# A convolution and a multiplicative feed-forward on one core: the first side task gets another tile, fewer sums, and a later place for its first product

## The chip, the cores and the metric

The kernel runs on one core of a Trainium2 chip. The metric is the time of one execution in microseconds of device time; where several executions were timed, the median is given. TensorE is PE in the profile, VectorE DVE, ScalarE ACT, GpSimd POOL, SyncE SP. A name such as L454 is line 454 of the kernel's file.

## The reference

x has the shape 8 x 3904 x 192, `weight` 8 x 7, and the four matrices of the feed-forward are 192 x 1024 (w1 and w2), 1024 x 1024 (w3) and 1024 x 192 (w_out). Each of 8 heads owns 24 of the 192 channels; its seven taps go through a softmax, and each channel is a causal sum of seven neighbouring tokens:

```
out[b, s, h, g] = sum_k softmax(weight)[h, k] * x_pad[b, s + k, h, g]
a = y @ w1;  b = y @ w2;  h = (a * b) @ w3;  result = h @ w_out
```

Here y is the convolution's result as 31232 rows of 192. Sums of the convolution start anew at the head of each of the 8 sequences.

## The kernel before, in words

**Rounds.** The 31232 tokens are two halves of 15616 (`NS = 2`), which run side by side: a half sits on 64 of the 128 partitions. A half is cut into 31 rounds R of 512 tokens, the last one shorter. w3 and w_out are multiplied together once (`w3_turn`, `w3_product`), into `W_sb`, so a round has two parts. `first_product(R)` (line 512) makes the products a and b for eight blocks of 128 columns, `pa` and `pb` in PSUM; ACT evicts `pa` (line 519) and DVE multiplies it with `pb` (line 521) into `abT`. `second_product(R, r)` multiplies `abT` with `W_sb` (line 537) for one half; ACT evicts the result into `osb` (line 542), and a DMA on SP's queue stores it. All of them take PSUM tiles from one pool of four (`banks`).

**Phases.** The order is written out by hand. Rounds 0 to 2 come first, with the conversion of the weights between them. Then phase p holds the first products of two rounds, and behind these the four second products of two earlier rounds. Phase 0 has only second products (rounds 0 and 1); phase 1 begins with rounds 3 and 4. Between the second products stand convolution units (`convolve`) where `places` names the phase and the position.

**Two ways to the convolution.** For most rounds the convolution is a banded matrix product on PE (`conv`, line 323), evicted as `convo` (line 332), stored as rows to DRAM (`store`, line 361) and brought back transposed into `xT` (`transposes`, line 395), all on SP's DMA queue. For six phases (`SIDE = (3, 7, 8, 11, 12, 14)`) it is done beside PE instead. There are 18 side tasks, three groups of 64 channels for each such phase. For task i, `side_cast` (line 438, POOL's queue) writes x in bf16 to DRAM, `side_transpose` (line 448, SP's queue) brings it transposed into a raw tile of 1040 columns, `side_first` (line 454, ACT) makes the product with one tap into the accumulator `acc_of[i % 2]`, and six sums on DVE (line 472) add the other taps, the last of them writing the operand `side_of`. The operand must be complete when the first products of its phase begin.

**Tiles of the side tasks.** Five raw tiles rotate. Four lie in the two places of the turned w3 tiles (`raw_of[0]` to `raw_of[3]`), the fifth behind the operand tile in the place of the first w3 load (`raw_of[4]`). The two accumulators lie in the places of two more w3 loads. So none of them is free before the weights have been worked up, which ends in round 2.

**The plan.** A loop gives each phase some sums (`room`: 8 where the phase has convolution units, else 7) and fills them in task order; a task may be split over two phases. Casts and transposes of a task are placed one phase ahead of its first product: the transposes of `starts[p + 1]` stand on SP's queue behind the first products of phase p. The first product of a task carries a number n: it is issued at the head of the n-th of the phase's four second products, and the sums behind it are issued from there on (`side_steps`). Every engine and every DMA queue runs its instructions in the order in which they were issued.

**Around the end of round 2** the order on SP's queue is: the taps, the transposes of the tasks of phase 0, the store of block 3 (rows that round 3 and round 4 need), the transposes of these two rounds into `xT`, and then the transposes of the tasks of phase 1. On POOL's queue, `later_loads` issues the weights, the casts of phase 0's tasks, the x rows of block 4, the casts of phase 1's tasks, and part of block 5. A DMA on SP's queue also waits for the eighth one before it to have landed.

Of the kernel before, what the change touches and what calls it, by code (L numbers as in the profile page):

```python
# [16 lines left out]
def kernel(  # L17
# [19 lines left out]
    NS = 2  # L37
# [31 lines left out]
    t0 = (LAG + 3) * CH  # L69
# [36 lines left out]
    rows_c = dram.tile([TS, NP, NS * Q], BF16, name="rows_c")  # L106
# [14 lines left out]
    def group(r, e):  # L121
        return slice((2 * r + e) * C, (2 * r + e) * C + C)
# [55 lines left out]
    for r in range(NS):  # L178
        p = group(r, 0).start
# [12 lines left out]
        out=diag, in_=diag, pattern=[[-1, 128 + 8]], compare_op=ALU.is_equal,  # L192
# [13 lines left out]
    for i in range(4):  # L206
        d = diag[i * C:i * C + C, i * C + 2 * i:i * C + 2 * i + C]
        nc.vector.tensor_copy(
            out=cmask[i * C:i * C + C],
            in_=bass.AP(tensor=d.tensor, offset=d.offset, ap=[d.ap[0], [1, 2], [1, C]]))  # L210
# [40 lines left out]
    for i in range(3):  # L251
# [3 lines left out]
        out=share[:, :, 0:K], in0=taps.unsqueeze(1).to_broadcast([H, H, K]), scalar=total,  # L255
        in1=diag[0:H, 0:H].unsqueeze(2).to_broadcast([H, H, K]), op0=ALU.mult, op1=ALU.mult)
    spread = banks("spread")
    for i in range(4):
# [6 lines left out]
        out=wsb, in_=spread[:, 0, 0:2 * H].rearrange("p (h k) -> p h k", h=H)  # L265
# [5 lines left out]
        out=cprod.rearrange("p h k (s two) -> p h k s two", two=2),  # L271
# [6 lines left out]
    p = group(1, 0).start  # L278
# [3 lines left out]
    for k in range(2):  # L282
# [5 lines left out]
                          in_=bps[:, 0, 0:C * H].rearrange("p (h s) -> p h s", s=C))  # L288
# [110 lines left out]
    HALO = 16  # L399
# [12 lines left out]
    def side_span(p):  # L412
        return (2 * p + 1) * CH, min((2 * p + 3) * CH, TS)

    tasks = [(q, k) for q in SIDE for k in range(NP)]
    side_of, acc_of, raw_of = {}, [], []
# [27 lines left out]
    def side_transpose(i):  # L444
        p, k = tasks[i]
        t0, t1 = side_span(p)
        for lo, hi in ((t0 - HALO, t0 + CH), (t0 + CH, t1)):
            nc.sync.dma_start_transpose(
                out=raw_of[i % 5][:, HALO + lo - t0:HALO + hi - t0], in_=rows_c[lo:hi, k, :])

    def side_first(i):
        p, k = tasks[i]
        t0, t1 = side_span(p)
        nc.scalar.activation(  # L454
            out=acc_of[i % 2][:, 0:t1 - t0], in_=raw_of[i % 5][:, HALO - 1:HALO - 1 + t1 - t0],
            func=ACT.Copy, scale=wC[:, k, K - 2:K - 1])

    def side_sums(i):
        p, k = tasks[i]
        t0, t1 = side_span(p)  # L460
        starts = [z for z in range(0, TS, S) if t0 <= z < t1]

        def job(d, last):
            def run():
                raw, acc = raw_of[i % 5], acc_of[i % 2]
                if d == 2:
                    for z in starts:
                        nc.vector.memset(acc[:, z - t0:z - t0 + 1], 0.0)
                for lo, hi in [(t0, t1)] if last else \
                        zip([t0] + [z + d for z in starts], starts + [t1]):  # L470
                    a = acc[:, lo - t0:hi - t0]
                    nc.vector.scalar_tensor_tensor(  # L472
                        out=side_of[p][:, k, 0:t1 - t0] if last else a,
                        in0=raw[:, HALO + lo - t0 - d:HALO + hi - t0 - d],
                        scalar=wC[:, k, K - 1 - d:K - d], in1=a, op0=ALU.mult, op1=ALU.add)
            return run
        size = (t1 - t0) / (2 * CH)
        return [(size, job(d, d == 0)) for d in list(range(2, K)) + [0]]
# [151 lines left out]
    for k in (0, 2, 1):  # L630
# [6 lines left out]
    places = {0: (0, 1), 1: (2,), 2: (0, 1, 2), 3: (0,), 4: (0,), 6: (0, 2), 7: (0, 2),  # L637
              10: (0,), 11: (0,)}
    starts, chain, room, p = {}, {}, 0, -1
    for i, (q, k) in enumerate(tasks):  # L640
        for cost, f in side_sums(i):
            while room < cost:
                p += 1
                room = 8 if p in places else 7
                at, free = 0, 0
                starts.setdefault(p, [])
            if not chain or chain[max(chain)][-1][0] != i:
                starts[p].append(i)
                n = min(2 * NS - 1, -int(-free * 0.48))
                chain.setdefault(p, []).append((i, n, lambda i=i: side_first(i)))  # L650
            assert p < q
            room, at = room - cost, at + cost
            chain.setdefault(p, []).append((i, None, f))
        free = at
    for p in starts:
        for i in starts[p]:
            assert i < 5 or p < 2 or max(v for v in chain if chain[v][0][0] <= i - 5) <= p - 2
# [20 lines left out]
    def later_loads():  # L678
# [12 lines left out]
        for f in x_jobs(5, 0):  # L691
# [16 lines left out]
        4: seq((w3_product, 4), (w3_product, 6),  # L708
               (conv, 3, 96, 96, (A,), (0,)), (conv, 3, 96, 96, (V,), (1,)),
               (A, wC[Q:128], wC[0:Q]), (side_tiles,), *[(side_transpose, i) for i in starts[0]],  # L710
               (store, 3), (transposes, 3), (transposes, 4))})

# [31 lines left out]
    for p, rounds in enumerate(phases):  # L744
# [16 lines left out]
        for i in starts.get(p + 1, ()):  # L761
            side_transpose(i)
# [44 lines left out]
```

## Time and profile before

| | |
|---|---|
| median of 3 runs | 518.94 us (517.76 to 519.64) |
| the profiled execution | 520.86 us, of which 519.2 are the span |
| PE busy | 510.7 us (98%) |
| DVE busy | 446.5 us (86%) |
| ACT busy | 353.3 us (68%) |
| POOL busy | 87.4 us (17%) |
| mean granted clock of TensorE | 0.997 |

The span runs from the first instruction to the last one of the profiled execution. Rows of a timeline give the start, the time taken, the engine and the line, what is written and read with its shape, how many instructions are merged, and in brackets how long the engine had been idle and what ended it. SPq is SP's DMA queue: its times are those of issuing, not of the transfer. A row of a window gives for each engine its busy time, then the granted clock, the share of the DMA engines and the GB/s. A row of a DMA queue gives packets, MB and a share of busy time.

### The profile page before, as it was taken

The page shows a single profiled execution, that of the slowest core. Times are in us where ns is not written, and L with a number is a line of the kernel's source. Part 1 is how long each engine was busy: PE and PEld are TensorE (multiplying, and loading weights), DVE is VectorE, ACT ScalarE, POOL GpSimd, SP SyncE. Part 2 cuts the span into 40 slices and gives each one's busy share as a digit, 9 for nine tenths or more (in the row PEclk, how much of TensorE's full clock was granted, in tenths as well). Part 3 has the DMA queues.
Part 4 walks back from the last instruction along what each step waited for, and adds up shares of the span by engine and source line. Part 5 has one row for each costly group of instructions (what it writes and reads, how often), then busy time and mean ns, then how long its engine had stood idle before and what let it go on. Part 6 is the DMA issues. An engine that isn't in the chain of part 4 may idle for free.

```text
span 519.2 us, 14128 instructions
## 1 busy us (share of the span) xinstructions
PE 510.7 (98%) x6020; PEld 336.4 (65%) x6020; DVE 446.5 (86%) x430; ACT 353.3 (68%) x403; POOL 87.4 (17%) x178
## 2 busy tenths in 40 slices
PE   8999889999999999999999999999999999999997
PEld 4446845846658476485765847658585585856777
DVE  6898679999899898989989899898998989989580
ACT  6886647577876776747777675684767667576462
POOL 9875013050030211302112021100000000000000
PEclk9999989999999999999999999999999999999999
DMA  9999959899697968937457499744013072210304
GB/s 143 150 154 173 162 126 213 158 138 120 134 174 144 156 84 179 155 101 80 58 114 55 107 175 172 152 59 133 7 56 100 2 181 64 64 61 3 123 2 153
DMA packets 154189, 59.46 MB, mean 115 GB/s; under 512 B 108945, under 2 KB 154125, under 8 KB 154125
## 3 DMA queue, kind: packets, MB, share of 16 engines
q0 software_dynamic: 66912, 17.07, 36.7%
q1 hardware_dynamic: 87053, 41.38, 35.6%
q8 instruction: 47, 0.77, 0.6%
q14 instruction: 17, 0.14, 0.1%
q10 hardware_dynamic: 160, 0.10, 0.1%
HBM read 34.42 MB, written 34.88 MB: 133 GB/s over the span
## 4 chain that ended last, share of the span: by engine, by line
PE 92%; DMA 3%; ACT 2%; DVE 1%; SPq 1%; issue 0%
PE pa L512 30%; PE pb L512 30%; PE ops L537 28%; DMA rows<-convo 2%; PE cps L323 2%; PE wps L605 1%; ACT asb L519 1%; ACT convo L332 1%; DVE abT L521 1%; PE warm L233 1%; SPq L395 1%; DMA xT<-rows 1%; DMA out_dram<-osb 0%; PE ops L558 0%; PE tps L385 0%
## 5 line engine op out<-in xcount | busy, mean ns | idle before, releaser
L521 DVE TENSOR_TENSOR abT<-asb,pb 128x1024 bf16<-128x1024 bf16 x240 | 292.5, 1221 | 45.3 <-ACT asb L519 27.4
L519 ACT CAST asb<-pa 128x1024 bf16<-128x1024 f32 x244 | 247.0, 1013 | 67.3 <-PE pa L512 66.9
L512 PEld LDWEIGHTS <-wn 64*128 64x128 bf16 x1488 | 139.0, 95 | 85.7 <-issue 3.6
L512 PEld LDWEIGHTS <-ws 64*128 64x128 bf16 x1488 | 131.1, 94 | 73.0 <-issue 3.3
L537 PE MATMUL ops<-W_sb,abT 128*128 128x192 bf16 x1936 | 164.8, 247 | 0.2 <-ACT convo L332 0.2
L537 PEld LDWEIGHTS <-abT 128*128 128x128 bf16 x1936 | 158.3, 98 | 8.0 <-issue 7.6
L512 PE MATMUL pa<-xT,wn 64*128 64x512 bf16 x456 | 124.1, 378 | 2.0 <-DMA xT<-rows 0.9
L512 PE MATMUL pb<-xT,wn 64*128 64x512 bf16 x456 | 125.2, 379 | 0.0
L512 PE MATMUL pa<-xT,ws 64*128 64x512 bf16 x456 | 124.2, 379 | 0.3 <-DMA xT<-rows 0.3
L512 PE MATMUL pb<-xT,ws 64*128 64x512 bf16 x456 | 123.0, 379 | 0.0
L542 ACT COPY osb<-ops 128x768 f32<-128x768 f32 (+1 forms) x61 | 48.6, 796 | 82.0 <-PE ops L537 82.0
L472 DVE SCALAR_TENSOR_TENSOR acc<-raw,wC,acc 128x1024 f32<-128x1024 bf16 (+3 forms) x100 | 93.9, 973 | 1.3
L512 PE MATMUL pb<-side,wn 64*128 64x512 bf16 (+1 forms) x288 | 75.0, 368 | 0.2 <-DVE abT L521 0.2
L512 PE MATMUL pa<-side,wn 64*128 64x512 bf16 (+1 forms) x288 | 74.5, 368 | 0.0
L512 PE MATMUL pa<-side,ws 64*128 64x512 bf16 (+1 forms) x288 | 74.4, 368 | 0.0
L512 PE MATMUL pb<-side,ws 64*128 64x512 bf16 (+1 forms) x288 | 73.7, 368 | 0.0
L749 POOL COPY pace<-abT 1x2 bf16<-1x2 bf16 x46 | 8.0, 174 | 221.8 <-DVE abT L521 221.8
L332 ACT CAST convo<-cps 128x640 bf16<-128x640 f32 (+2 forms) x62 | 34.1, 633 | 1.8 <-PE cps L323 1.7
L157 POOL DMA_DIRECT2D xb<-in_x_dram x46 | 30.3, 663 | 9.6 <-issue 6.4
L438 POOL DMA_DIRECT2D rows_c<-in_x_dram x36 | 27.4, 763 | 9.7 <-issue 8.9
L472 DVE SCALAR_TENSOR_TENSOR acc<-side,wC,acc 128x1024 f32<-128x1024 bf16 (+6 forms) x20 | 19.5, 1013 | 1.9 <-ACT acc L454 1.6
L454 ACT ACTIVATE acc<-raw,wC 128x1024 f32<-128x1024 bf16 (+1 forms) x15 | 16.8, 1117 | 4.5 <-DMA raw<-rows_c 4.5
(68 smaller groups left out, 126.2 us busy)
## 6 DMA issues: line engine op xcount, KB each, us to landing
out_dram<-osb SPq DMA_DIRECT2D x58, 384.0 KB
xb<-in_x_dram POOLq DMA_DIRECT2D x28, 240.0 KB, 7.0
rows_c<-in_x_dram POOLq DMA_DIRECT2D x30, 130.0 KB, 3.8
rows<-convo SPq DMA_DIRECT2D x13, 120.0 KB
rows<-convo SPq DMA_DIRECT2D x6, 240.0 KB
xb<-in_x_dram POOLq DMA_DIRECT2D x6, 228.0 KB, 8.2
w3b<-in_moe_w_dram POOLq DMA_DIRECT2D x4, 256.0 KB, 5.6
w3b<-in_moe_w_dram POOLq DMA_DIRECT2D x8, 128.0 KB, 5.8
```

Source lines behind the costliest of these rows:

```text
L157: nc.gpsimd.dma_start(out=tiles[js[0]][0][group(r, e), s:s + w, :], in_=bass.AP(tensor=x.tensor, offset=(r * TS + t - PAD) * D, ap=[[D, C] ...
L323: nc.tensor.matmul(o.rearrange("p (w g) -> p w g", g=wd)[:, :, c - c0:c1 - c0], Aband[group(r, e), h, :], xb[group(r, e), s:s + m, c:c1], ...
L332: f(out=convo[:, e::E, k, :, lo:lo + c] .rearrange("p w r g -> p r w g"), in_=src[:, :, :, o:o + c])
L438: nc.gpsimd.dma_start(out=rows_c[t0 - HALO:t1, k, r * Q:r * Q + Q], in_=x_rows[r * TS + t0 - HALO:r * TS + t1, k * Q:k * Q + Q])
L454: nc.scalar.activation(out=acc_of[i % 2][:, 0:t1 - t0], in_=raw_of[i % 5][:, HALO - 1:HALO - 1 + t1 - t0], func=ACT.Copy, scale=wC[:, k, K ...
L472: nc.vector.scalar_tensor_tensor(out=side_of[p][:, k, 0:t1 - t0] if last else a, in0=raw[:, HALO + lo - t0 - d:HALO + hi - t0 - d], scalar ...
L512: nc.tensor.matmul(p[:, r, f * N:f * N + N], w_of(i, k, r)[rs, ft * 128:(ft + 1) * 128], operand(R, k, rs), start=(k == 0), stop=(k == NP ...
L519: nc.scalar.copy(out=asb[:, :, 0:per * N], in_=pa[:, :, 0:per * N])
L521: nc.vector.tensor_tensor(out=ab[:, f0, :, 0:N], in0=asb[:, :, 0:N], in1=pb[:, :, 0:N], op=ALU.mult)
L537: nc.tensor.matmul(ops[:, g // 2, (g % 2) * D:(g % 2) * D + D], ab[:, jt, r, g * 128:(g + 1) * 128], W_sb[:, jt, :], start=(jt == 0), stop ...
L542: nc.scalar.copy(out=osb.rearrange("p (a g) d -> p a (g d)", g=2), in_=ops[:, 0:ng // 2, 0:2 * D])
L749: P(out=pace, in_=abT_of[R][0:1, ft, 1, 0:2])
```

## The change

Three edits, all in the side tasks.

```
-                out=raw_of[i % 5][:, HALO + lo - t0:HALO + hi - t0], in_=rows_c[lo:hi, k, :])
+                out=raw_of[i % 5 - 1][:, HALO + lo - t0:HALO + hi - t0], in_=rows_c[lo:hi, k, :])
...
-                room = 8 if p in places else 7
-                at, free = 0, 0
+                room = 5 if p == 0 else 8 if p in places else 7
+                at, ends = 0, {}
...
-                n = min(2 * NS - 1, -int(-free * 0.48))
+                n = max(p == 0, -(-ends.get(i - 2, 0) // 2))
...
-        free = at
+        ends[i] = at
```

The index `i % 5 - 1` stands in `side_first` and `side_sums` too. It shifts the rotation by one: task 0 takes `raw_of[4]`, in the place of the first w3 load, and tasks 1 to 4 take the four tiles in the places of the turned w3.

Phase 0 gets five sums instead of eight. So it holds only task 0, without its last sum; its transposes are the only side transposes ahead of the store of block 3, and those of tasks 1 and 2 come one place later on SP's queue, behind the transposes of rounds 3 and 4. On POOL's queue the casts of task 1 move behind the x rows of block 4. Every later sum moves back by three, so that phases 8 and 12 hold other tasks than before, and the last sums of task 14 and of task 17 are now the last ones of phases 11 and 13.

The number n of a task's first product came from the number of sums that the phase had taken before it. It is now half of the number of sums at which the task before last, which has the same accumulator, ended within this phase, and 0 where that task ended earlier. In phase 0 it is at least 1. By this, all products stand at the head of their phase, but for task 0 (ahead of the second of phase 0's second products) and tasks 2 and 6 (at the same place in phases 1 and 4).

PE's instructions and their order are the same.

More of the change, by code (lines that the diff above doesn't have):

```diff
@@ L454, in side_first @@
         nc.scalar.activation(
-            out=acc_of[i % 2][:, 0:t1 - t0], in_=raw_of[i % 5][:, HALO - 1:HALO - 1 + t1 - t0],
+            out=acc_of[i % 2][:, 0:t1 - t0], in_=raw_of[i % 5 - 1][:, HALO - 1:HALO - 1 + t1 - t0],
             func=ACT.Copy, scale=wC[:, k, K - 2:K - 1])
@@ L464, in run @@
             def run():
-                raw, acc = raw_of[i % 5], acc_of[i % 2]
+                raw, acc = raw_of[i % 5 - 1], acc_of[i % 2]
                 if d == 2:
```

## The prediction

> **What bounds the kernel now.** I read the page's span, engine shares and clock row first, then the chain that ended last, and then the timeline of the stretch in which that chain leaves TensorE (PE).
>
> ```profile
> span 519.2 us, 14128 instructions
> ```
>
> ```profile
> PE 510.7 (98%) x6020; PEld 336.4 (65%) x6020; DVE 446.5 (86%) x430; ACT 353.3 (68%) x403; POOL 87.4 (17%) x178
> ```
>
> ```profile
> PEclk9999989999999999999999999999999999999999
> ```
>
> PE is busy for 98% of the span, so the time moves only where PE waits or runs at a lower clock. The clock row has one dip, in the sixth slice (65 to 78 us). The chain's longest pieces (start, us, what) give the clean length of a phase and the place where PE leaves the chain; the row after them is the timeline's, the start of phase 0:
>
> ```profile
> 53.84 9.53 DMA rows<-convo
> 91.47 8.03 PE ops L537 x96
> ...
> 220.81 10.67 PE ops L537 x128
> 252.31 2.75 PE ops L537 x32
> ...
> 285.09 2.75 PE ops L537 x32
> ...
> 317.50 10.66 PE ops L537 x128
> ```
>
> ```profile
> 52.45 2.82 PE L537 MATMUL ops<-W_sb,abT 128*128 128x192 bf16 x32
> ```
>
> From the second products of phase 5 (220.81), which have no convolution unit among them, to those of phase 6 (252.31) it is 31.50 us: 10.67 for the four and 20.83 for the pair of first products. Phase 0 has two convolution units of 0.7 each more (row below), so 12.1 and 20.83. It began at 52.45; undisturbed, the second products of phase 1 would start at 85.4. They start at 91.47: **6.1 us are lost here**, and nearly nothing later. Where, by the timelines of PE, ACT and SP's DMA queue:
>
> ```profile
> 59.13 0.22 PE L323 MATMUL cps<-xb,Aband 32*32 32x120 bf16 x2 [0.46 <-ACT osb L542]
> 60.05 0.70 PE L323 MATMUL cps<-xb,Aband 32*32 32x120 bf16 x62 [0.69 <-ACT convo L332]
> ...
> 67.28 0.37 PE L512 MATMUL pa<-xT,wn 64*128 64x512 bf16 x1 [0.87 <-ACT osb L542]
> ...
> 68.01 0.37 PE L512 MATMUL pa<-xT,ws 64*128 64x512 bf16 x1 [0.33 <-DMA xT<-rows]
> ...
> 69.32 0.37 PE L512 MATMUL pa<-xT,wn 64*128 64x512 bf16 x1 [0.92 <-DMA xT<-rows]
> ```
>
> ```profile
> 57.24 1.15 ACT L454 ACTIVATE acc<-raw,wC 128x1024 f32<-128x1024 bf16 x1 [4.53 <-DMA raw<-rows_c]
> 58.30 0.78 ACT L542 COPY osb<-ops 128x768 f32<-128x768 f32 x1
> 58.98 1.94 ACT L332 CAST convo<-cps 128x640 bf16<-128x640 f32 x4
> ```
>
> ```profile
> 46.36 5.85 SPq L448 DMA_TRANSPOSE raw<-rows_c  x4
> 52.33 8.54 SPq L361 DMA_DIRECT2D rows<-convo  x8
> 61.06 0.31 SPq L354 DMA_DIRECT2D rows<-convo  x1
> 63.39 7.08 SPq L395 DMA_TRANSPOSE xT<-rows  x5
> ```
>
> Two things hold PE. First, the side product of task 0 stands ahead of the first eviction in ACT's queue and waits 4.53 us for its raw tile. The eviction runs only at 58.30, PE runs out of PSUM tiles, and the second unit is through at 60.75 instead of about 58.5: 2.3 us. Second, round 3's operand is late. The store of its rows starts at 52.33 behind four side transposes, a part of it lands 9.53 us after 53.84, and only then do the transposes into xT start (63.39; the third has landed when PE goes on at 69.32). The waits ended at 67.28, 68.01 and 69.32 come to 2.1 us. (The first is put down to an eviction; the tile it needs was free by then, so I read it as xT's first landing.) Then the clock is down, 70 to 72 in the window view:
>
> ```profile
> 70.00:72.00 2.00, 2.00 (x14) 0.80 (x10) 1.00 (x1) 0.76 (x1) 0.00 (x0) 0.50 0.33 74
> ```
>
> The granted clock, third from the end, is 0.50. The pace of the matmuls says that this lasts from 69.5 to 72.8, so some 1.6 us are lost. 2.3 + 2.1 + 1.6 = 6.0, which closes on the 6.1.
>
> **The change, part by part.** *Raw tile of task 0 in w3's first place.* Its first transpose now waits until 46.36 for a turned w3 tile to be multiplied. The new place is free after the second turn, and then the two casts decide:
>
> ```profile
> 38.95 1.24 DVE L594 STREAM_TRANSPOSE w3T<-w3b 128x1024 f32<-128x1024 f32 x1
> ...
> 48.39 1.22 DVE L332 CAST convo<-cps 128x320 bf16<-128x320 f32 x2 [1.45 <-PE cps L323]
> ```
>
> ```profile
> L438 POOL DMA_DIRECT2D rows_c<-in_x_dram x2: 793/795/797, 35.1 to 35.9; - x2
> ```
>
> ```profile
> DMA to landing us min/median/max: 8.1/8.1/8.2
> ```
>
> The turn ends at 40.19, the second cast lands at 35.9 + 8.1 = 44.0, and both casts keep their place in POOL's order. So the transposes go out at 44.0, 2.4 us sooner.
>
> *Five sums in phase 0, so only task 0 is fetched ahead.* Two of the four side transposes leave the queue ahead of the store. The other two hold SP for half of 5.85 us, to 47.0; the store then waits only for its data, evicted by 49.61 (48.39 + 1.22), and starts 2.7 us sooner. When it lands is the one large unknown. Queue rows (packets, MB, busy share) of 48 to 50, where SP's queue has no row at all, and of 50 to 52:
>
> ```profile
> q0 software_dynamic: 1872, 0.33, 210.6%
> ```
>
> ```profile
> q0 software_dynamic: 1068, 0.26, 132.8%
> q1 hardware_dynamic: 348, 0.09, 33.4%
> ```
>
> So the transposes issued from 46.36 on moved nothing before 50. Call T the moment at which the transposes into xT can go out (63.39 now). Early end: packets start 4 us after issue as now, at 48, move at some 200 per us, about 1,040 for two transposes (0.27 MB at 0.09 for 348), until 53.2; the 0.39 MB of the four stores that round 3 needs follow at the same packet rate with rows of 768 bytes (2.5 us), and I allow 1.4 us until they count as landed: T = 57.1. Late end: nothing moves before 50.5 whatever is queued, the two transposes end at 55.7, and the stores get only 0.12 MB per us (3.2 us): T = 60.3. The third operand is there 69.32 - 63.39 = 5.9 later, at 63.0 to 66.2. PE, undisturbed, wants it at 52.45 + 12.1 + 0.43 = 65.0, since four matmuls of a group precede it. I take the middle, 64.6, which costs nothing, and charge 0.4 us for the late half.
>
> *The product behind the first eviction.* ACT would evict at about 55.3, cast the first unit by 58.1 and then run the product, 1.15 us. Its tile is there even if it lands as late as now, 57.24. The second unit finds its PSUM tiles free. The five sums behind the product end near 66, when the first eviction of round 3 is made. Were that cover gone, each sum too many would cost its own 1.3 us.
>
> *What moves elsewhere.* Task 1's casts go behind the four x loads of block 4 on POOL: these loads get earlier, and the tile is wanted in phase 1 only. Tasks 1 and 2 put four transposes behind those into xT, where task 2's two stood, so half of 5.85 more stands ahead of the output stores, block 4's store and round 5's transposes:
>
> ```profile
> 90.69 6.96 SPq L395 DMA_TRANSPOSE xT<-rows  x4
> ```
>
> Round 5's third transpose was out by 90.69. With 4.7 less from T, 2.9 more and 4 to land it is there by 92.9, and PE now wants it at about 96.5: hidden, with over 3 us left.
>
> *Later products, and sums that end later.* A product now goes out as soon as its accumulator is free, mostly at the head of a phase, where ACT idles before the first eviction. In phase 6 one stands ahead of the last eviction: 252.31 to 285.09 takes 32.78 us, against 32.41 for phase 7 (to 317.50) with as many units. Those 0.37 us go. In return, three sums have slid back through the schedule, and task 14's last sum becomes the eighth of phase 11, wanted at once by phase 12:
>
> ```profile
> 414.32 5.24 DVE L472 SCALAR_TENSOR_TENSOR acc<-side,wC,acc 128x1024 f32<-128x1024 bf16 x4
> ```
>
> ```profile
> 424.18 0.75 PE pa L512 x6
> ```
>
> Eight at 5.24 / 4 = 1.31 from 414.32 end at 424.8; PE wants the result at 424.18 + 0.43 = 424.6: 0.2 us lost. Phase 13 has nine sums of 768 columns at its end, three quarters as long (8.8 us, begun about 1.6 after PE's second products): inside their 10.67, nothing lost.
>
> **The sum.** 6.1 + 0.37 - 0.2 - 0.4 = 5.9 us, against the profiled execution's 520.86 (519.2 of span and 1.7 around it). That one stood 1.9 above the median of the runs, 518.94; the gain is taken as the same there: **513.0**.
>
> **The rivals.**
>
> *A: part of the operand's lateness stays.* For it: 9.53 us from issue to landing is far more than a store's own packets. Against it: two transposes fewer ahead of it. With T at 61.2, PE waits 2.1 us at 65.0. If the clock falls again as at 70 to 72, 1.6 more goes: gain 6.3 - 2.1 - 1.6 = 2.6, 516.3; without that, 4.2 and 514.7. In the rows the dip followed three short waits, broken by matmuls, so I price A with the dip. [...]
>
> *B: the store is held by the software queue, not by the transposes ahead of it.* For it: nothing moved for SP in 48 to 50 beside that queue's 1872 packets. Then T stays near 63.4, PE arrives at 64.6 and is held to 69.32 as now, with the dip: the front gains nothing, 0.37 less 0.2 is left: 518.8. Against it: in 50 to 52 both queues moved, and what SP's moved were transposes, not the store. [...]
>
> *C, slower: the raw tile comes late, now behind the first eviction.* There it holds the second eviction, the second unit's casts and the PSUM tile of the fourth second product, due at 61.8. If the tile lands at L, PE goes on at L + 1.15 + 0.78, a loss of L - 59.9. That equals today's 6.1 at L = 66.0 and is slower by over 0.3% from 67.6; at 69 the time is 521.8. Against it: L is 57.24 now, with a later issue.
>
> **How the numbers follow.** The forecast (T up to about 60) has 0.68, A 0.18, B 0.09, C 0.05. About 0.3%, 1.6 us, is what a measurement of this kernel can tell. Faster are the forecast and A, 0.86; the same is B, 0.09; slower is C, 0.05. The forecast's own range is 511.7 to 514.7: gains of 6.3 to 5.1 between the ends of T, and 0.9 either way as the three runs spread. Reaching over A's priced end with some spread: 511.7 to 516.8.
>
> **What would show it.** Right: task 0's product on ACT follows the first eviction near 58 with no wait; the store starts near 49.7; the transposes into xT go out by 60.3; PE's waits at 59.13 and 67.28 are gone, no slice has a lower clock, and phase 1's second products start near 85.6. Phase 6 to 7 takes 32.4. Wrong: transposes into xT still near 63, a wait for raw behind the first eviction, or PE held by a side sum at the head of phase 12 or 14 for over 1 us.

## The result and the profile after

The changed kernel takes 515.82 us (median of 6 runs, 515.41 to 517.49) against 518.80 for the kernel before in the same comparison: a ratio of 0.9948, with a 95% interval of 0.9930 to 0.9966. It is faster by 3.0 us. The time lies inside the prediction's outer range, 511.7 to 516.8, but above the forecast's own, 511.7 to 514.7, and the gain is half of the 5.9 us forecast. By the number alone it would be taken for rival A (514.7 to 516.3); the rows below say otherwise. Its profiled execution took 516.07, with a span of 514.4.

On the page, PE is busy for 99% of the span, and the dip of the granted clock is gone:

```profile
PE 508.4 (99%) x6020; PEld 335.9 (65%) x6020; DVE 446.5 (87%) x430; ACT 353.6 (69%) x403; POOL 87.7 (17%) x180
```

```profile
PEclk9999999999999999999999999999999999999999
```

The timelines of SP's queue, ACT and PE around phase 0, in that order, and the chain's piece that begins phase 1's second products:

```profile
43.64 2.52 SPq L448 DMA_TRANSPOSE side<-rows_c  x2
50.53 3.19 SPq L361 DMA_DIRECT2D rows<-convo  x8
57.32 0.32 SPq L354 DMA_DIRECT2D rows<-convo  x1
59.63 8.73 SPq L395 DMA_TRANSPOSE xT<-rows  x6
```

```profile
56.14 0.80 ACT L542 COPY osb<-ops 128x768 f32<-128x768 f32 x1 [2.58 <-PE ops L537]
56.84 1.96 ACT L332 CAST convo<-cps 128x640 bf16<-128x640 f32 x4
58.64 1.19 ACT L454 ACTIVATE acc<-side,wC 128x1024 f32<-128x1024 bf16 x1
59.69 0.83 ACT L542 COPY osb<-ops 128x768 f32<-128x768 f32 x1
```

```profile
53.29 2.81 PE L537 MATMUL ops<-W_sb,abT 128*128 128x192 bf16 x32
56.03 0.73 PE L323 MATMUL cps<-xb,Aband 32*32 32x120 bf16 x64
56.69 2.81 PE L537 MATMUL ops<-W_sb,abT 128*128 128x192 bf16 x32
59.44 0.72 PE L323 MATMUL cps<-xb,Aband 32*32 32x120 bf16 x64
60.10 5.45 PE L537 MATMUL ops<-W_sb,abT 128*128 128x192 bf16 x64
```

```profile
86.38 8.03 PE ops L537 x96
```

The reader is to see three things. The product (L454) runs behind the first eviction with no wait. Two transposes instead of four stand ahead of the store, and those into xT go out at 59.63. PE has no bracket left in this stretch: phase 0 begins at 53.29 and phase 1's second products at 86.38, **33.09 us** later, where the profiled execution before had 39.02. In this front part the waits are gone as forecast.

The rest of the two traces, by the same starts of second products (32.78 and 32.41 for phases 6 and 7 before):

```profile
247.28 2.75 PE ops L537 x32
...
279.70 2.75 PE ops L537 x32
...
312.48 10.67 PE ops L537 x128
```

Phase 6 to 7 takes 32.42 now, so the 0.37 went there; but 7 to 8 takes 32.78, so it came back. From phase 10 to 12 it is 64.74 (375.48 to 440.22) against 64.51 before: 0.23 lost at task 14's last sum. And phase 0 begins 0.84 later in this execution (53.29 against 52.45). 5.93 + 0.36 - 0.37 - 0.23 - 0.84 = 4.85, the difference of the two spans, 4.8. The late start is not the work of the instructions that were moved: it stands in the chain ahead of them all, as the landing of the first load of x; PE's first convolution waits 0.84 us for it, and the later rounds keep that distance:

```profile
2.31 4.90 DMA xb<-in_x_dram
...
7.25 0.71 PE cps L323 x61
```

So the two profiled executions differ by what was forecast, less 0.4 in phase 7 and a late start; the medians differ by 3.0. The question for the experiments is which of the two tells the truth, and which of the edits carries it.

### The profile page after: what moved, and what is told of

Its sections match the earlier page's. It is cut to its first block, busy times and chain, and to the rows that moved or that the text cites. A ratio compares the mean times of both kernels' runs of the same rounds, so it can differ in the third digit from the quotient of the medians.

```text
span 514.4 us, 14129 instructions
## 1 busy us (share of the span) xinstructions
PE 508.4 (99%) x6020; PEld 335.9 (65%) x6020; DVE 446.5 (87%) x430; ACT 353.6 (69%) x403; POOL 87.7 (17%) x180
## 4 chain that ended last, share of the span: by engine, by line
PE 93%; DVE 3%; ACT 1%; DMA 1%; issue 1%; POOL 0%; POOLq 0%
PE pa L512 30%; PE pb L512 30%; PE ops L537 30%; PE cps L323 2%; DVE acc L472 1%; DVE abT L521 1%; PE wps L605 1%; DMA xb<-in_x_dram 1%; ACT asb L519 1%; ACT convo L332 0%; DVE side L472 0%; PE ops L558 0%; PE tps L385 0%; PE tps L370 0%; POOL xb L157 0%
## 5 line engine op out<-in xcount | busy, mean ns | idle before, releaser
L512 PE MATMUL pb<-xT,ws 64*128 64x512 bf16 x456 | 121.7, 376 | 0.0
L472 DVE SCALAR_TENSOR_TENSOR acc<-raw,wC,acc 128x1024 f32<-128x1024 bf16 (+3 forms) x90 | 88.4, 1014 | 1.2
L472 DVE SCALAR_TENSOR_TENSOR acc<-side,wC,acc 128x320 f32<-128x320 bf16 (+13 forms) x30 | 24.9, 879 | 0.3
L472 DVE SCALAR_TENSOR_TENSOR side<-raw,wC,acc 128x1024 bf16<-128x1024 bf16 (+1 forms) x14 | 17.4, 1246 | 0.5
```

Of the source, the lines that this page charges most:

```text
L472: nc.vector.scalar_tensor_tensor(out=side_of[p][:, k, 0:t1 - t0] if last else a, in0=raw[:, HALO + lo - t0 - d:HALO + hi - t0 - d], scalar ...
L512: nc.tensor.matmul(p[:, r, f * N:f * N + N], w_of(i, k, r)[rs, ft * 128:(ft + 1) * 128], operand(R, k, rs), start=(k == 0), stop=(k == NP ...
```

## The experiments

Each was timed in five rounds beside the kernel before. "Phase 0" below means the time from the start of its second products to those of phase 1, read from the trace as above; without any wait it is 33.1. "xT at" is the time at which SP issues the first transpose into xT. A median is to be read beside that of the kernel before in the same comparison: 518.49 for e1 to e4, 518.37 for e5 to e8, 518.64 for e9 to e11, 518.51 for e12. The ratio is an estimate over all executions, so it is not exactly the quotient of the two medians.

| kernel | median us | ratio to before, 95% | phase 0 | xT at |
|---|---|---|---|---|
| before, profiled at first | 518.80 | | 39.02 | 63.39 |
| e1, before again | 518.08 | 0.9991 (0.9968 to 1.0013) | 35.98 | 61.36 |
| e2, tile only | 517.25 | 0.9974 (0.9954 to 0.9994) | 34.91 | 61.21 |
| e3, five sums only | 517.27 | 0.9972 (0.9949 to 0.9995) | 34.86 | 59.87 |
| e4, product behind only | 520.41 | 1.0030 (1.0010 to 1.0049) | 38.07 | 61.87 |
| changed | 515.82 | 0.9948 (0.9930 to 0.9966) | 33.09 | 59.63 |
| e9, changed again | 515.44 | 0.9929 (0.9905 to 0.9953) | 33.08 | 57.50 |
| e5, changed, product first | 515.61 | 0.9941 (0.9919 to 0.9963) | 33.21 | 57.92 |
| e6, changed, old tile | 515.85 | 0.9966 (0.9945 to 0.9986) | 33.08 | 59.24 |
| e7, changed, eight sums | 518.09 | 0.9992 (0.9976 to 1.0008) | 36.20 | 61.23 |
| e12, changed, two tasks ahead | 517.66 | 0.9972 (0.9945 to 0.9999) | 34.26 | 61.21 |
| e8, changed, six sums | 515.32 | 0.9936 (0.9914 to 0.9958) | 33.54 | 57.49 |
| e10, e8 again | 515.21 | 0.9924 (0.9898 to 0.9950) | 33.54 | 58.87 |
| e11, changed, old places later on | 515.74 | 0.9934 (0.9910 to 0.9958) | 33.08 | 57.52 |

### e1: the kernel before, once more

No edit.

> The kernel before, unchanged, to see how its executions spread and what phase 0 costs in another profiled one. Theory D: the 6.1 us that phase 0 lost in the profiled execution were a dear draw; 1.6 of them, the low clock behind the waits, come only in some executions. Then executions with a mean clock of 1.000 take 517.5 to 519, those at 0.997 take 520 to 521, and in a profiled execution at 1.000 the second products of phase 1 start about 37.4 us after those of phase 0 instead of 39.0. Rival S: phase 0 loses about 6 in every execution (39.0 in the new profile too, whatever the clock), and the changed kernel gives some 2 to 3 us back elsewhere in most executions.

Its profiled execution took 517.73, with a mean clock of 1.000. Timelines of ACT, SP and PE, the chain, and a window (granted clock third from the end):

```profile
56.88 1.15 ACT L454 ACTIVATE acc<-raw,wC 128x1024 f32<-128x1024 bf16 x1 [4.31 <-DMA raw<-rows_c]
```

```profile
61.36 8.18 SPq L395 DMA_TRANSPOSE xT<-rows  x6
```

```profile
52.30 2.81 PE L537 MATMUL ops<-W_sb,abT 128*128 128x192 bf16 x32
```

```profile
67.81 0.37 PE L512 MATMUL pa<-xT,wn 64*128 64x512 bf16 x1 [0.34 <-DMA xT<-rows]
```

```profile
88.28 8.03 PE ops L537 x96
```

```profile
68.00:72.00 4.00, 4.00 (x40) 2.20 (x38) 3.40 (x4) 3.04 (x3) 0.13 (x1) 1.00 0.44 99
```

The wait of ACT is the same (4.31 against 4.53), but the transposes into xT go out 2.0 us sooner than in the first profile, PE waits less for them, and the clock stays at full speed. Phase 0 costs 35.98, so **2.9 us over the clean 33.1, not 6**. Theory D had said 37.4, so even it saw too little of the spread. (This execution is one of the quicker ones: the median of its twelve is 518.08.) Over the 98 executions of the kernel before in these comparisons for which a clock is known, most lie between 517.3 and 519.1 at a mean clock of 1.000; in 21 the clock was 0.997 or lower, and nearly all of these took 519 to 523. The execution that the prediction was made from, 520.86 at 0.997, is not among the 98, but it is of the same kind as the 21. Rival S, a loss of about 6 us in every execution, falls.

### e2, e3, e4: each edit alone, on the kernel before

```
e2:  raw_of[i % 5]  ->  raw_of[i % 5 - 1]
e3:  room = 8 if p in places else 7  ->  room = 5 if p == 0 else 8 if p in places else 7
e4:  n = min(...)  ->  n = max(p == 0, min(...))
```

> The kernel before with the raw tiles shifted by one and nothing else: task 0 in w3's first place, both tasks still fetched ahead of the store. Theory (two causes: ACT's wait and the lateness of round 3's operand): the product no longer waits behind the raw tile, but four transposes stay ahead of the store, so the transposes into xT go out at 61 to 62; PE waits some 2 us there; 1 to 2 us faster than before. Rival O (only the operand's chain sets the end, and the number of transposes sets it): no faster than before by more than 0.5 us. Rival P (ACT's wait alone was the loss): as fast as the changed kernel, 3 us faster than before.

> The kernel before with five sums in phase 0 and nothing else: only task 0 is fetched ahead of the store, in its old tile, and its product stays ahead of the first eviction. Theory: the transposes into xT go out near 60 instead of 63.4, but ACT still waits for the raw tile until 56 to 57, so PE comes to round 3 some 2 us late: 1.5 to 2.5 us faster than before. Rival O: as fast as the changed kernel. Rival P: no faster than before by more than 0.5 us.

> The kernel before with task 0's product behind the first eviction and nothing else. Theory: PE no longer waits at 59 to 61, but the transposes into xT still go out at 63.4 and PE waits for them to 69.3 as before, now in one piece of some 4 us instead of several: within 0.7 us of before, rather slower if the longer wait brings the low clock each time (up to 1.6). Rival P: 2.3 us faster.

In e2 the product no longer waits, and the transposes into xT stay at 61.21. It is 1.2 us faster, as the two causes said. Its trace has one oddity, a stop of PE inside the fourth second product with no releaser in the profile. PE comes to round 3 only at 66.6 because of it, so a wait for xT may be hidden behind it; what the stop is stays open:

```profile
65.89 0.82 PE L537 MATMUL ops<-W_sb,abT 128*128 128x192 bf16 x8 [1.43 <-issue]
```

In e3 it is the other way round: the transposes go out at 59.87, and ACT still waits:

```profile
57.27 1.15 ACT L454 ACTIVATE acc<-raw,wC 128x1024 f32<-128x1024 bf16 x1 [4.60 <-DMA raw<-rows_c]
```

That leaves 34.86 - 33.1 = 1.8 us, the price of ACT's wait where the operand is early. The median is 1.2 us under before, less than the 1.5 to 2.5 expected (the interval reaches from 0.3 to 2.6). In e4 ACT's wait is gone and the operand is about as late as in e1 (transposes into xT at 61.87, not at the 63.4 expected). PE now waits for it almost in one piece, 0.54 and then 2.71 us, and the half clock follows:

```profile
68.87 0.58 PE L512 MATMUL pa<-xT,wn 64*128 64x512 bf16 x1 [2.71 <-DMA xT<-rows]
```

```profile
69.00:71.00 2.00, 2.00 (x12) 0.74 (x11) 1.14 (x3) 1.01 (x1) 0.00 (x0) 0.50 0.35 78
```

10 of e4's 12 executions were at 0.997 or lower, and it is **slower than before**, by 0.1 to 0.5% (1.9 us in the median; at most 1.6 had been expected). Beside e1, the four second products end 1.5 us sooner after phase 0's start (12.25 against 13.75), but the waits for xT come to 3.25 us instead of 1.05, and the clock takes more. So rival P, the ACT wait alone, falls by e2 and e4, and rival O, the operand alone, by e3: the intervals of e2 and e3 do not reach the 3 us of all edits together.

Both causes have to go. In e4, where only ACT's wait goes, the result is worse than nothing. e2 is not a second test of this: its early tile sends two of the four side transposes at 42.75, and the store begins at 50.22, where e4 has 46.56 and 52.32. So the tile helps the operand too.

### e5, e6: the changed kernel, one edit undone

```
e5:  n = max(p == 0, -(-ends.get(i - 2, 0) // 2))  ->  n = -(-ends.get(i - 2, 0) // 2)
e6:  raw_of[i % 5 - 1]  ->  raw_of[i % 5]
```

> The changed kernel with task 0's product back ahead of the first eviction of phase 0, all else as changed. Theory (the raw tile, sent early and with one task only, is there before ACT is free): in the changed kernel's trace the packets of the two transposes end near 52 and ACT is free at 53.6, so the product runs without a wait and the time is that of the changed kernel within 0.4 us; its place is worth nothing once the tile is early. Rival P (its place is what removes the stall): 1.5 to 2.3 us slower than the changed kernel, with an ACT wait on the raw tile of over 1 us in the trace.

> The changed kernel with the raw tiles in their old rotation: task 0's transposes wait for the turned w3 tile again (46 to 47 instead of 44). Theory: the product, behind the first eviction, is still covered (raw there at 57, wanted at 58.6); the stores stand behind transposes that end 2 us later, the transposes into xT go out near 60 to 60.5, the third operand is there about when PE wants it: 0 to 0.8 us slower than the changed kernel. Rival O (the earlier tile is what pulls the operand's chain forward): 2 us slower or more, with PE waiting on xT.

In e5 the product runs at the head of phase 0 without a wait:

```profile
52.84 1.15 ACT L454 ACTIVATE acc<-side,wC 128x1024 f32<-128x1024 bf16 x1
```

Phase 0 is 33.21 and the median that of the changed kernel. In e6 the transposes start at 46.24 again, the product behind the eviction is covered, and its profiled execution has the clean 33.08. So the tile and the place do the same work for ACT: with one task fetched ahead, either is enough. They are perhaps not quite equal. In e6, 5 of 12 executions took 517.5 to 519.5; in e5 none of 6 went above 515.9, and of the 12 of the changed kernel one took 517.5. With the transposes into xT at 59.24, e6 stands at the edge that the prediction had put at 59.1 (65.0 less 5.9); that its dearer executions fall over this edge was not traced.

### e7 and e12: two tasks ahead of the store

```
e7:   room = 5 if p == 0 else 8 if ...  ->  room = 8 if p in places else 7
e12:  casts and transposes of starts[0]  ->  of starts[0] + starts[1][:1]   (and starts[1][1:] later)
```

> The changed kernel with eight sums in phase 0 again: two tasks fetched ahead of the store, task 0 in the early tile, both products behind the first eviction. Theory: the four transposes ahead of the store put the transposes into xT at 61 to 62, PE arrives at 65 to 65.5 and waits for them till 67 to 68 in one piece, the clock falls in many executions: 2 to 3.5 us slower than the changed kernel, about as slow as the kernel before. Rival Q (the number of transposes ahead of the store does not matter, the software queue sets the store's landing): within 0.5 us of the changed kernel.

> The changed kernel with task 1's casts and transposes back ahead of the store, and all instructions of PE, ACT and VectorE as changed: five sums in phase 0, so VectorE is not late as it was with eight. Theory: the two further transposes alone put the transposes into xT at 60.5 to 61.5 instead of 57.5 to 59.6, PE comes to round 3 at 64.9 and waits 1 to 2 us for its third operand: phase 0 to phase 1 takes 34 to 35 us instead of 33.1, and the median is 1 to 2 us over the changed kernel's 515.4 to 515.8, with some executions at the low clock. Rival Q (the time to the landing of the store is the software queue's, and what the room of eight cost was VectorE's lateness): transposes into xT at 57.5 to 59.6 and phase 0 within 0.3 us of 33.1.

e7 puts the transposes into xT at 61.23 and gives the gain back. The rest of the expectation did not come: PE's waits for xT are two, 0.77 and 0.19 us, the clock of the profiled execution is 1.000, and only 2 of 12 executions were at 0.997. The trace shows a second cause instead, which the expectation had not named: with eight sums behind a later product VectorE comes late to round 3, and PE waits for it.

```profile
71.23 0.37 PE L512 MATMUL pb<-xT,wn 64*128 64x512 bf16 x1 [1.51 <-DVE abT L521]
```

So e12 leaves all sums as changed and moves only DMAs: task 1's transposes go ahead of the store, and its casts go ahead of block 4's x rows on POOL's queue. PE waits at one place:

```profile
61.21 8.63 SPq L395 DMA_TRANSPOSE xT<-rows  x6
```

```profile
65.86 0.37 PE L512 MATMUL pa<-xT,wn 64*128 64x512 bf16 x1 [0.71 <-DMA xT<-rows]
```

Phase 0 takes 34.26 in the profiled execution, 1.2 over the clean one; the median is 1.8 us over the changed kernel's, and 3 of 12 executions were at 0.997 or lower. One task more ahead of the store moves xT's transposes by 1.6 to 3.7 us against the two traces of the changed kernel (57.5 to 59.9 in all kernels with one task ahead, 61.2 to 63.4 with two) and decides over 1 to 2 us. SP's queue shows how: in e12 the store's first eight DMAs take 8.39 us to go out (50.13 to 58.52); in the changed kernel they take 3.19, none of them waits for a side transpose, and the last is out by 53.72. In the first profile of before, with four side transposes ahead as in e12, the eight take 8.54, and 3.7 of these are three waits for the landing of side transposes. Rival Q, by which xT's transposes would have stayed at 57.5 to 59.6, falls. What the place of the casts adds was not tried by itself.

### e9, e8, e10, e11: the changed kernel again, six sums, and the later places

```
e8, e10:  room = 5 if p == 0  ->  room = 6 if p == 0
e11:      n = max(p == 0, -(-ends.get(i - 2, 0) // 2))  ->  n = max(p == 0, min(2 * NS - 1, -int(-free * 0.48)))
```

> The changed kernel, unchanged, for more executions of it beside those of before. Theory D: the kernel before has a common execution, at 517.5 to 518.5, and a dearer one with the low clock in one of four or five, while the changed kernel has room ahead of round 3's operand and rarely pays it. So the median lies 2.5 to 3.0 us under that of before, executions at 0.997 are at most one in eight, and the profiled one again has 33.1 to 33.2 us from the second products of phase 0 to those of phase 1. Rival S (the changed kernel loses 2 to 3 us elsewhere in most executions): phase 0 at 33.1, but over 1 us lost at other phases than 7 and 11.

> The changed kernel with six sums in phase 0, so that task 0 is finished there and task 14 ends as the seventh sum of phase 11. Theory: phase 12's first products no longer wait for a side sum, 0.23 us less from the second products of phase 10 to those of phase 12; the sixth sum in phase 0 makes VectorE late for round 3 by up to 0.6 us, which PE's slack takes: 0.2 us faster than the changed kernel, too little for the timed runs to show, and to be read in the trace. Rival: the sixth sum is not covered, and phase 0 to phase 1 takes over 33.5 us instead of 33.1.

> The kernel with six sums in phase 0 once more, on the same chip as the changed kernel. By the first trace it loses 0.45 in phase 0 and gains 0.23 at phase 11 and 0.31 at phase 7 against the changed one: within 0.4 us of it, too near for the timed runs.

> The changed kernel with the later first products back at the places that the old rule gives them (half the sums that the phase has already taken), task 0's still behind the first eviction. It prices the last edit by itself. Theory: a product ahead of the last eviction of a phase costs 0.37 us, as in phase 6 of the kernel before, and the old rule now puts one there in two or three phases; elsewhere it is free: 0.3 to 1.2 us slower than the changed kernel. Rival: nothing, within 0.2 us, since the 0.37 came back in phase 7 of the changed kernel although no product stands there.

e9: 515.44, 3.2 us under before, all six executions at 0.999 or 1.000. With the first six, 1 of 12 executions of the changed kernel was at 0.997, against 21 of 98 before. Beside e1, trace against trace at full clock: phase 0 gains 2.90, phase 6 gains 0.37, phase 7 loses 0.35, phases 10 and 11 lose 0.24: 2.7 us. That is the gain between two ordinary executions, as far as two traces can tell; the spans differ by 2.3 only, since phase 0 begins 0.37 later in e9, a distance that is there by 22 us already (22.21 against 21.83), ahead of what was changed. The dear executions that the kernel before has now and then add to the gain.

e8 and e10 read as expected at phase 11 (64.51 from 10 to 12), but the sixth sum is not covered: phase 0 takes 33.54 both times, since PE waits for VectorE at round 3 (0.28 in its timeline). Phase 7's loss is not there (32.47), so the sum of the three is 0.1 us; the median is 0.2 us under e9 on the same chip, inside the noise. It has the lowest median here, but is not shown to be faster.

e11 costs 0.30 in the median against e9, all six of its executions above 515.6. In its trace 0.24 of it lies between phases 1 and 2 (32.20 against 31.96). One phase loses, then, not the two or three expected, and the last edit of the change is worth some 0.3 us.

## Why the prediction was wrong in size

**The mechanism was right.** Point by point: the transposes went out at 43.6 (44.0 forecast); the store began at 50.53, which is 49.7 as forecast and the 0.84 by which phase 0 began later; the transposes into xT at 59.63, with phase 0 starting 0.84 later, so 58.8 on the forecast's scale (58.7 its middle, 57.1 to 60.3 its ends); the product behind the first eviction ran without a wait; no wait and no low clock remained; phase 1's second products began 33.09 after phase 0's (33.0). Rivals A, B and C did not come. e12 is what A looks like, at a lower price: its transposes into xT go out at 61.21, and PE waits 0.71 us where A had 2.1.

**The step that failed is the last of the sum: "the gain is taken as the same there".** The loss was real (5.93 us against the changed kernel, 6.1 forecast), but it was read in an execution 2.1 us above the median of all runs (518.80). Such an excess has to lie somewhere, and it lay in the stall that was being priced: e1's ordinary execution loses 2.9 there, and 3.0 of the 3.2 us between the two spans lie in phase 0. Of the three terms, 2.3 for ACT's wait, 2.1 for xT and 1.6 for the clock, the clock's is 0 in about four of five executions, and the waits come to about 2.9 together with xT at 61.4 instead of 63.4. The prediction's own fence showed the clock dip, and the table above it the 1.9 between the profiled time and the median; put together they say that the gain at the median is 1.9 less or so, 4.0 and a time of 515. That was left undone. Of the 1.0 us between 4.0 and the 3.0 measured, phase 7 has 0.35; where the rest went is not shown. That 515.82 still lies inside the outer range is luck: the range was stretched to there for rival A, which did not come.

**The split of the loss was off as well.** The prediction let the second unit be through at about 58.5 without the wait on ACT. In the changed kernel it is through 6.87 us after phase 0's start (59.44 + 0.72 - 53.29), which is 59.3 on the scale of the first profile. By the end of the four second products the wait had cost 1.7 us (60.97 + 5.44 - 52.45 = 13.96, against 60.10 + 5.45 - 53.29 = 12.26), and e3 says 1.8, not 2.3. What is left for the clock, 5.93 - 1.7 - 2.1, is then 2.1 rather than 1.6. Part of that may not be the clock's, since e1, at a clock of 1.000, loses some 0.3 more than its two waits there: round 3's first six matmuls begin 2.05 us before the next group (65.98 to 68.03), where the groups behind them take 0.64 or 0.65 each and the waits are 1.05.

**The small terms.** Phase 6's 0.37 went, as forecast, but came back in phase 7 for another reason:

```profile
303.91 3.48 DVE L521 TENSOR_TENSOR abT<-asb,pb 128x1024 bf16<-128x1024 bf16 x3 [0.50 <-POOL pace L749]
```

VectorE waits 0.50 us for POOL's pacing copy, and PE feels 0.37 of it; the chain of that stretch leads from the copy through VectorE's product to PE:

```profile
303.55 0.18 POOL pace L749
...
303.91 1.23 DVE abT L521
...
305.18 0.82 PE pb L512 x6
```

The wait stands in the traces of the changed kernel, e3, e5, e6, e9 and e11, and not in those of e1, e2, e4, e7, e8, e10 and e12, of which e12 has the changed kernel's plan for ACT, VectorE and PE. What calls it up stays open. Task 14's sum was forecast at 0.2 and costs 0.23:

```profile
418.42 1.30 DVE side L472
...
419.76 0.39 PE pa L512 x2
```

Phase 13's nine sums cost nothing, as forecast, and the four transposes behind those into xT were hidden.

**The sign of a part.** The prediction priced the two causes as addends, 2.3 and 2.1 with the clock on top. For the change, which removes both, this did no harm. e4 shows that they are not addends: taking the first away alone moves PE into the second, where 2.71 us of waiting come in one piece and the clock falls in most executions.

## What to carry to other kernels

Before a stall is priced from one profile, hold that execution against the median and its clock against 1.000: an execution above the median has its excess somewhere, and here it was the stall that was being looked at. Where two late things end at the same place, remove the one that ends last first: removing the earlier one alone cost 1.9 us in e4, since the whole wait then fell on PE at once. And what is fetched ahead on an ordered queue should be only what is wanted first: here one task more put off the transposes behind the store by 1.6 to 3.7 us.

## What the runs showed of the hardware

**The clock fell after waits of 3.25 and of 2.1 us.** In e4's profile, PE waits 0.54 and 2.71 us with four matmuls between them, and the granted clock is then 0.50 from 69 to 71, 0.57 over 70 to 72 and 0.82 over 71 to 73: half the speed until about 71.7, as groups of six matmuls begin 1.28 us apart at 69.25 and 70.53, and 0.65 apart from 71.76 on. In 10 of its 12 executions the mean clock was 0.997 or lower. In the first profile of before the clock fell after three waits of 2.1 us together (0.50 over 70 to 72); in e1 it did not after two of 1.05 (1.00 over 68 to 72).

**The side transposes moved some 4 us after their issue, beside a busy software queue.** In the changed kernel they were issued at 43.64, and the mass of their packets moved in 48 to 52, as in the kernel before (46.36, and 50 on). The rows of the two queues in 48 to 50:

```profile
q0 software_dynamic: 782, 0.10, 174.4%
q1 hardware_dynamic: 520, 0.13, 49.6%
```

The lag of some 4 us is what the prediction's early end had assumed. No run here has these transposes without traffic on the software queue, so that this traffic causes the lag is not shown.
